# Top-32 attention and two MLPs on one core: more buffers for raw weights, shared memory for two stages, one more mask on ScalarE

## The chip, the cores and the metric

The kernel runs on 1 core of one Trainium2 chip. The metric is the device time of one execution in microseconds (us), the median of several runs. Below, PE is TensorE's matmul, PEld its weight load, DVE is VectorE, ACT is ScalarE, POOL is GpSimd and SP is SyncE, which issues the DMAs here.

## The reference

```python
# q, k, v: (4 batches, 8 heads, 576, 64); w_in: 512x2048, w_out: 2048x512, twice
scores = (q @ k^T) / 8
kth = the 32nd largest score of each row
attn = softmax of the scores >= kth, the others left out
x = (attn @ v), heads side by side: 2304 x 512
h = x @ w_in;  x = (h - tanh(h)) @ w_out
h = x @ w2_in; out = where(h > 0, h, exp(min(h, 0)) - 1) @ w2_out
```

## The kernel before

The 2304 tokens are six chunks of 384 (`CHUNKS`). Attention of a chunk is cut into 8 groups of three 128-row score tiles: chunk 0 is groups 0 to 7, chunk 1 groups 8 to 15, chunk 2 groups 16 to 23. A tile's top 32 are found on VectorE by four MAX8 (`find`, line 395) with three MATCH_REPLACE8 between them (`drop`, line 409). Then the mask: for most tiles ScalarE has taken the exponentials early (line 399) and VectorE multiplies them by `score >= 32nd` and sums (line 416, SCALAR_TENSOR_TENSOR). For the first `MASK_ACT[chunk]` tiles of a group ScalarE does it alone instead: after GpSimd has made two small constants (lines 401 to 403), a Prelu with a huge slope (line 411) and an Exp that sums (line 412). Before, that is three of three tiles in chunk 0, one in chunk 1, none later.

The two MLPs work in fp32r with each operand as a high and a low part, so every weight is prepared once. `prepare` loads 128x512 int64 words of raw weights (`wr`, 4 KB a partition, `RAW_BUFS` buffers). ScalarE reads them twice (lines 189 and 190), GpSimd once (line 192), VectorE joins the pieces (`wf`, line 195), ScalarE and GpSimd split that into high and low (`wp`, lines 142 and 143), and a DMA stores the pair to DRAM (line 200). There are 64 such halves: (MLP 0 or 1, 16 blocks, in or out). Blocks 12 to 21 (`EARLY`) are stored and read back, the others are used at once by chunk 0 too; later chunks read all from DRAM (line 211). While attention of chunk 0 runs, the first 26 halves take a PSUM bank for one piece (`"wide" in stage`), and the other 38 do not.

An MLP step is `first` (12 matmuls into `h`, line 566), tanh or exp on ScalarE, `gate` (VectorE, lines 580 and 585; then `gh` on ScalarE and `gl` on GpSimd, lines 142 and 143) and `second` (9 matmuls into three `acc` banks, line 602). Chunk c's steps run beside attention of chunk c+1.

Attention scores of chunk 2 are made ahead, in the stretch before the first MLP step. For 24 tiles `park` makes the scores on PE (`pp`, line 360), ScalarE copies them (`sp`, line 343, two buffers) and a DMA takes them to DRAM (`sd`, line 345). All 24 must be through before the first `h`, and before the first two transposes of chunk 0's last group (`hurried`), because `bank("h")` first closes the PSUM pool of `pp`.

Everything is written in program order by ticks, four to a group, and a list scheduler then sets the order on each engine by simulated time and priority. Each engine runs its own list strictly in order. Parks carry a low priority (`PARK_LOW`).

Of the kernel before, what the change touches and what calls it, by code (L numbers as in the profile page):

```python
# [19 lines left out]
P = 128  # L20
B, H, S, D = 4, 8, 576, 64
# [7 lines left out]
NF = DFF // P  # L29
# [13 lines left out]
SIZES = [sum(n for _, _, n in c) for c in CHUNKS]  # L43
NMAX = max(SIZES)

MASK_ACT = [3, 1, 0, 0, 0, 0]

GATE_GP = [0, 0, 1, 1, 1, 2]

# [19 lines left out]
PARK_BUFS = 2  # L69
# [18 lines left out]
G_BUFS = 3  # L88
T_BUFS = 3
# [9 lines left out]
NU = 384  # L99
# [8 lines left out]
def tile_topk_attention_two_mlps(  # L108
# [58 lines left out]
    weights, loads = {}, [(ci, m, ft) for ci in range(len(SIZES)) for m in range(2) for ft in range(NF)]  # L167

    def weight_tile(half, name):
        return sb.tile([P, 2, 512], F32R, tag=f"w{half}", name=name, bufs=(WI_BUFS, WO_BUFS)[half])  # L170

    stage = {"at": 0, "wide": True}

    def prepare(m, ft, half):

        raw = sb.tile([P, 512], I64, tag="wr", name=f"wr{m}_{ft}_{half}", bufs=RAW_BUFS)
        nc.sync.dma_start(raw, (w1, w2)[m][ft][:, half * 512 : half * 512 + 512])  # L180
        words = raw.bitcast(F32).rearrange("p (n w) -> p n w", w=2)
        w = sb.tile([P, 512], F32, tag="wf", name=f"wf{m}_{ft}_{half}", bufs=2)
        low, scaled = words.bitcast(U32)[:, :, 0], words[:, :, 1]
        small = scaled
        if "wide" in stage:
            small = bank(f"acc{stage['at'] % 3}", f"sc{m}_{ft}_{half}", 1)
            stage["at"] += 1
        if small is not scaled:
            nc.scalar.activation(small, scaled, copy, scale=2.0**-112)
        nc.scalar.activation(low.bitcast(I32), low, copy, scale=2.0**-29 * (1 - 2.0**-20), bias=-0.5 + 7.5 * 2.0**-20)  # L190
# [4 lines left out]
        nc.vector.scalar_tensor_tensor(  # L195
            w.bitcast(U32), small.bitcast(U32), 3, low, op0=ALU.logical_shift_left, op1=ALU.bitwise_or
        )
        wt = weight_tile(half, f"wp{m}_{ft}_{half}")
        split(wt[:, 0], wt[:, 1], w)
        nc.sync.dma_start(f(scratch[m, ft, half]), f(wt))  # L200
        return wt

    def load_next():
        if loads:
            ci, m, ft = loads.pop(0)
            for half in range(2):
                if ci == 0 and m * NF + ft not in EARLY:
                    weights[ci, m, ft, half] = prepare(m, ft, half)
# [13 lines left out]
    for ci, size in enumerate(SIZES):  # L222
        for p in range(NPAIR):
            row = []
            c0 = 0
            for b, q0, n in CHUNKS[ci]:
                for heads in ([[0], [1]] if n >= 256 else [[0, 1]]):
                    u = Unit()
# [10 lines left out]
            cuts, k = [], 0  # L239
# [7 lines left out]
            for us in cuts:  # L247
                g = Group()
# [19 lines left out]
    def parked(u):  # L268

        return u.g.at in PARK  # L270

    pair_k = {}

    def wide(u):

        return u.whole or parked(u)

    def load_q(u):
        if wide(u):
            h = u.heads[0]  # L280
            tag, bufs = ("qp", 1) if parked(u) else ("qraw", QR_BUFS)
            u.qraw = sb.tile([P, NU], F32, tag=tag, name=f"qw{u.id}", bufs=bufs)
            nc.gpsimd.memset(u.qraw[(1 - h) * D : (2 - h) * D, : u.n], 0.0)
            nc.sync.dma_start(u.qraw[h * D : h * D + D, : u.n], qT[u.b, 2 * u.p + h, :, u.q0 : u.q0 + u.n])
            return
        u.qraw = sb.tile([P, NU], F32, tag="qraw", name=f"qraw{u.id}", bufs=QR_BUFS)
        src = qT[u.b, 2 * u.p + u.heads[0] : 2 * u.p + u.heads[-1] + 1, :, u.q0 : u.q0 + u.n].rearrange("h d s -> d h s")
        nq = u.n * len(u.heads)
        for half in range(2):
            nc.sync.dma_start(u.qraw[half * D : half * D + D, :nq].rearrange("d (h s) -> d h s", s=u.n), src)  # L290

# [263 lines left out]
    def first(ci, m, ft):  # L555
        n = SIZES[ci]
        xh, xl = x_tiles[ci] if m == 0 else z_tiles[ci]
        h = bank("h", f"h{ci}_{m}_{ft}", 2)[:, :n]
        wv = weights.pop((ci, m, ft, 0)).rearrange("p a (k c) -> p a k c", c=P)
        jobs = [(wi, xs, kt) for wi, xs in ((0, xh), (1, xh), (0, xl)) for kt in range(4)]  # L560
        if m == 0 and ft == 0:
            jobs.sort(key=lambda x: x[2])
        late = (n // P - 1) * P
        for cs in (slice(0, late), slice(late, n)) if m == 1 and ft < PARTED and late else (slice(0, n),):
            for a, (wi, xs, kt) in enumerate(jobs):
                nc.tensor.matmul(h[:, cs], wv[:, wi, kt], xs[:, kt, cs], start=(a == 0), stop=(a == len(jobs) - 1))  # L566
# [152 lines left out]
    early = list(EARLY)  # L719
    for tick in range(FIRST_TICK, n_ticks):  # L720
# [18 lines left out]
        at, r = divmod(tick, 4)  # L739
# [63 lines left out]
```

## Time and profile before

| what | us |
|---|---|
| median of 3 runs (1238.9 to 1240.79) | 1240.16 |
| the profiled execution | 1244.14 |
| its span, first to last instruction | 1242.4 |
| PE busy in the span | 1156.3 (93%) |
| PEld | 981.6 (79%) |
| DVE | 973.8 (78%) |
| ACT | 761.9 (61%) |
| POOL | 584.3 (47%) |

Busy time is the union of an engine's instructions. Each engine's share changes from stage to stage: PE's is low up to about 186 us, where the first MLP steps begin, and DVE's falls to nearly nothing from 1055 us, when attention is done. A matmul's record reaches from its issue to its end and overlaps its neighbours, so a PE that is busy all the time can still be waited for in small pieces.

### The profile page before, as it was taken

How to read it: one execution, taken by the hardware profiler on the slowest of the kernel's cores; microseconds unless marked ns; L12 is line 12 of the kernel's file. 1: busy time of each engine (PE TensorE's matmuls, PEld its weight loads, DVE VectorE, ACT ScalarE, POOL GpSimd, SP SyncE). 2: the span in 40 equal slices, each digit the busy share in tenths (PEclk: the TensorE clock that was granted, in tenths of full speed). 3: DMA queues.
4: the chain of work that ended last, by engine and by line, in shares of the span. 5: the costliest groups of instructions: out<-in, count | busy, mean ns of one | idle time of the engine just before them, and what ended most of it. 6: DMA issues, size and time to landing. Idle time of an engine off the chain costs nothing.

```text
span 1242.4 us, 19713 instructions
## 1 busy us (share of the span) xinstructions
PE 1156.3 (93%) x6349; PEld 981.6 (79%) x6349; DVE 973.8 (78%) x1951; ACT 761.9 (61%) x1646; POOL 584.3 (47%) x629
## 2 busy tenths in 40 slices
PE   6577669999889999999999999999999999999998
PEld 4344358888778887988888989989998988889887
DVE  6989989999999999969879679899789997100111
ACT  5899987787885435645556556566565564432333
POOL 4677758965975222244423345435244413333221
PEclk8788788999999999999999999999999999999999
DMA  7899947795779986778857779787778766687672
GB/s 244 313 318 339 300 147 243 255 364 185 269 273 381 310 240 186 249 222 251 238 180 231 238 227 262 209 277 215 242 239 252 197 163 199 205 282 252 219 251 80
DMA packets 115464, 302.83 MB, mean 244 GB/s; under 512 B 22560, under 2 KB 39840, under 8 KB 115360
## 3 DMA queue, kind: packets, MB, share of 16 engines
q1 hardware_dynamic: 115360, 301.56, 76.9%
q8 instruction: 51, 0.84, 0.3%
q14 instruction: 53, 0.43, 0.1%
HBM read 256.11 MB, written 45.39 MB: 243 GB/s over the span
## 4 chain that ended last, share of the span: by engine, by line
PE 70%; DMA 9%; ACT 8%; DVE 7%; POOL 2%; issue 2%; SPq 1%; ACTq 0%; POOLq 0%; DVEq 0%
PE h L566 28%; PE acc L602 28%; DMA wr<-in_w_dram 6%; PE av L459 5%; PE pt L437 4%; DVE vm L395 3%; DVE w L409 2%; PE ps L372 2%; PE ps L373 2%; DVE wf L195 1%; PE ps L360 1%; ACT s L374 1%; DVE e L416 1%; ACT wr L190 1%; POOL wr L192 1%
## 5 line engine op out<-in xcount | busy, mean ns | idle before, releaser
L143 POOL TENSOR_TENSOR gl<-g,gh 128x384 fp32r<-128x384 f32 x192 | 204.1, 1065 | 360.5 <-ACT gh L142 343.7
L395 DVE MAX8 vm<-w 128x8 f32<-128x576 f32 x432 | 317.3, 749 | 2.9
L602 PE MATMUL acc<-wt,gh 128*128 128x512 f32 x1020 | 271.6, 397 | 0.8 <-ACT gh L142 0.8
L602 PEld LDWEIGHTS acc<-wt,gh 128*128 128x128 f32 x1020 | 187.2, 188 | 36.2 <-issue 2.7
L409 DVE MATCH_REPLACE8 w<-vm,w 128x576 f32<-128x576 f32 x288 | 213.0, 741 | 0.0
L580 DVE SCALAR_TENSOR_TENSOR g<-t,h 128x384 f32<-128x384 f32 x96 | 52.3, 545 | 126.8 <-ACT t L572 124.4
L566 PE MATMUL h<-zh,wt 128*128 128x384 f32 (+2 forms) x784 | 148.0, 324 | 2.3 <-ACT zh L621 1.5
L602 PE MATMUL acc<-wt,gl 128*128 128x512 f32 x510 | 149.6, 398 | 0.0
L142 ACT ACTIVATE gh<-g 128x384 fp32r<-128x384 f32 x192 | 100.5, 525 | 74.6 <-DVE g L580 38.4
L566 PE MATMUL h<-xh,wt 128*128 128x384 f32 x672 | 142.1, 339 | 1.9 <-DVE g L580 1.5
L566 PEld LDWEIGHTS h<-zh,wt 128*128 128x128 f32 x784 | 126.7, 188 | 8.8 <-ACT zh L621 2.7
L438 ACT ACTIVATE ph<-pt 116x384 f32<-116x384 f32 (+1 forms) x240 | 110.2, 496 | 34.0 <-PE pt L437 33.3
L395 DVE MAX8 vm<-s 128x8 f32<-128x576 f32 x144 | 106.8, 750 | 29.6 <-ACT s L374 29.1
L374 ACT ACTIVATE s<-ps 128x288 f32<-128x288 f32 (+1 forms) x272 | 105.7, 415 | 38.0 <-PE ps L373 30.7
L437 PE MATMUL pt<-ident,e 128*116 128x128 f32 (+1 forms) x720 | 114.1, 286 | 14.7 <-ACT e L412 6.0
L566 PEld LDWEIGHTS h<-xh,wt 128*128 128x128 f32 x672 | 117.6, 188 | 8.8 <-DVE g L580 1.8
L571 ACT ACTIVATE t<-h 128x384 f32<-128x384 f32 x96 | 46.7, 488 | 118.3 <-PE h L566 116.3
L437 PEld LDWEIGHTS pt<-ident,e 128*116 128x116 f32 (+1 forms) x720 | 88.2, 140 | 35.8 <-ACT e L412 9.7
L416 DVE SCALAR_TENSOR_TENSOR e<-s,vm,e 128x576 f32<-128x576 f32 x115 | 111.8, 980 | 2.7 <-ACT e L399 2.2
L569 ACT ACTIVATE t<-h 128x384 f32<-128x384 f32 x96 | 47.0, 491 | 104.5 <-PE h L566 104.4
L602 PEld LDWEIGHTS acc<-wt,gl 128*128 128x128 f32 x510 | 93.6, 188 | 18.5 <-POOL gl L143 0.2
L409 DVE MATCH_REPLACE8 w<-vm,s 128x576 f32<-128x576 f32 x144 | 106.6, 741 | 0.0
(84 smaller groups left out, 2001.4 us busy)
## 6 DMA issues: line engine op xcount, KB each, us to landing
wt<-w SPq DMA_DIRECT2D x340, 512.0 KB, 4.9
wr<-in_w_dram SPq DMA_DIRECT2D x64, 512.0 KB, 5.7
w<-wp SPq DMA_DIRECT2D x64, 512.0 KB, 5.3
kraw<-in_kT_dram SPq DMA_DIRECT2D x96, 144.0 KB, 4.7
vraw<-in_vL_dram SPq DMA_DIRECT2D x64, 160.0 KB, 3.7
sd<-sp SPq DMA_DIRECT2D x24, 288.0 KB, 4.9
s<-sd SPq DMA_DIRECT2D x24, 288.0 KB, 6.7
qraw<-in_qT_dram SPq DMA_DIRECT2D x64, 96.0 KB, 4.0
```

Source lines behind the costliest of these rows:

```text
L142: nc.scalar.activation(hi, src, copy)
L143: return nc.gpsimd.tensor_sub(lo, src, f(hi))
L374: nc.scalar.activation(s[lo:hi, cs], pt[lo:hi, :HS], copy)
L395: nc.vector.max(g.vm[:, j, min(r, 1)], u.s[t] if r == 0 else g.w[j])
L409: nc.vector.match_replace(g.w[j], v, u.s[t] if r == 0 else g.w[j], FILL)
L416: nc.vector.scalar_tensor_tensor(u.e[t], u.s[t], v[:, 7:8], u.e[t], op0=ALU.is_ge, op1=ALU.mult, accum_out=g.sum[:, j : j + 1])
L437: nc.tensor.transpose(pt[:kn, j * P : j * P + P], v.e[t][:, k0 : k0 + kn], ident)
L438: nc.scalar.activation(g.ph[:kn, blk, :nq], pt[:kn, :nq], copy)
L459: nc.tensor.matmul(banks[c0][h * D : h * D + D, : v.n], v.vraw[h][:kn, blk], v.g.ph[:kn, blk, cs], start=(blk == order[0]), stop=(blk == o ...
L566: nc.tensor.matmul(h[:, cs], wv[:, wi, kt], xs[:, kt, cs], start=(a == 0), stop=(a == len(jobs) - 1))
L580: nc.vector.scalar_tensor_tensor(g, t, -1.0, h, op0=ALU.add, op1=ALU.max)
L602: nc.tensor.matmul(acc[ci, m][t], gx[:, t * P : t * P + P], wt[:, wi], start=(ft == 0 and k == 0), stop=(ft == NF - 1 and k == 2),)
```

## The change

Three things. `RAW_BUFS` goes from 3 to 5. To make room, tiles that only live before the first MLP step (`qp`, `kp`, `sp`) move to a pool of their own, which is closed when the first MLP tile is asked for; a pool with the MLP's `t`, `g`, `gh` and `gl` then takes the same memory. And `MASK_ACT[1]` goes from 1 to 2. `OPEN_BUFS` is 0, so its branch is never taken, and `prepare` is cut into three functions that issue the same instructions.

```diff
-MASK_ACT = [3, 1, 0, 0, 0, 0]
+MASK_ACT = [3, 2, 0, 0, 0, 0]
+OPEN_BUFS = 0
-RAW_BUFS = 3
+RAW_BUFS = 5
...
+    opening = ExitStack()
+    pools = {"open": opening.enter_context(tc.tile_pool(name="op", bufs=1))}
+
+    def mlp_tile(shape, dt, **kw):
+        if "open" in pools:
+            opening.close()
+            del pools["open"]
+            pools["mlp"] = pool("mlp", 1)
+        return pools["mlp"].tile(shape, dt, **kw)
...
-            u.qraw = sb.tile([P, NU], F32, tag=tag, name=f"qw{u.id}", bufs=bufs)
+            u.qraw = (pools["open"] if parked(u) else sb).tile([P, NU], F32, tag=tag, name=f"qw{u.id}", bufs=bufs)
...
-        s = sb.tile([P, S], F32, tag="sp", name=f"sp{u.id}_{t}", bufs=PARK_BUFS)
+        s = pools["open"].tile([P, S], F32, tag="sp", name=f"sp{u.id}_{t}", bufs=PARK_BUFS)
...
-        t = sb.tile([P, NMAX], F32, tag="t", name=f"t{ci}_{m}_{ft}", bufs=T_BUFS)[:, :n]
+        t = mlp_tile([P, NMAX], F32, tag="t", name=f"t{ci}_{m}_{ft}", bufs=T_BUFS)[:, :n]
```

(`kp` is changed as `qp` is, and `g`, `gh` and `gl` as `t` is.) The scheduler answers with another order up to about the end of chunk 2's attention; behind that each engine's list is the same as before. Three places show it. Line numbers of the change's rows are those of the changed file.

SP, the first raw loads (`wr0_13_0` is MLP 0, block 13, half 0; `sd` are the parks' stores). Before:

```order
L325 DMA vraw0_1_0_0_0_0_497<-in_vL_dram 128x320
L180 DMA wr0_13_0_502<-in_w1_dram 128x512
L325 DMA vraw0_1_0_0_1_1_701<-in_vL_dram 128x320
L284 DMA qw0_1_0_0_0_212<-in_qT_dram 64x384
L345 DMA sd2_0_1_192_0_0_291<-sp2_0_1_192_0_0_286 128x576
L345 DMA sd2_0_1_192_0_1_324<-sp2_0_1_192_0_1_319 128x576
L180 DMA wr0_13_1_514<-in_w1_dram 128x512
```

Now:

```order
L352 DMA vraw0_1_0_0_0_0_500<-in_vL_dram 128x320
L195 DMA wr0_13_0_505<-in_w1_dram 128x512
L195 DMA wr0_13_1_517<-in_w1_dram 128x512
L195 DMA wr0_14_0_624<-in_w1_dram 128x512
L352 DMA vraw0_1_0_0_1_1_704<-in_vL_dram 128x320
L311 DMA qw0_1_0_0_0_215<-in_qT_dram 64x384
L372 DMA sd2_0_1_192_0_0_294<-sp2_0_1_192_0_0_289 128x576
L372 DMA sd2_0_1_192_0_1_327<-sp2_0_1_192_0_1_322 128x576
L195 DMA wr0_14_1_636<-in_w1_dram 128x512
```

Two raw loads more are issued ahead of the first parks' stores. With the loads the joins on VectorE move up: the join of `wf0_5_1`, the 35th half of the list, stands 206th in VectorE's list before and 182nd now, and still 36 halves are joined before the first MLP gate in both.

PE, at the transposes of chunk 0's last group (`pt0_3_0_3_0_0_1_0` and `..._1_1` are its blocks 0 and 1, `pp2_3_1_192_1_2` is the last park). Before, the last park stands at row 171, 29 rows ahead of block 0:

```order
L372 MATMUL ps1_0_0_384_0_0_0_0_1335<-kk1_0_0_384_0_0_1234,qs1_0_0_384_0_1231 128x288
L373 MATMUL ps1_0_0_384_0_0_0_0_1335<-kk1_0_0_384_0_0_1234,qs1_0_0_384_0_1231 128x288
L372 MATMUL ps1_0_0_384_0_0_1_0_1339<-kk1_0_0_384_0_0_1234,qs1_0_0_384_0_1231 128x288
L373 MATMUL ps1_0_0_384_0_0_1_0_1339<-kk1_0_0_384_0_0_1234,qs1_0_0_384_0_1231 128x288
L437 MATMUL pt0_3_0_3_0_0_1_0_1563<-ident_69,e0_3_0_0_1_0_1370 116x128
L437 MATMUL pt0_3_0_3_0_0_1_1_1568<-ident_69,e0_3_0_0_1_0_1370 116x128
L437 MATMUL pt0_3_0_3_0_0_1_2_1573<-ident_69,e0_3_0_0_1_0_1370 116x128
```

Now:

```order
L387 MATMUL pp2_3_1_192_1_2_1459<-kw2_3_1_192_0_1037,qw2_3_1_192_1_1152 128x288 x2
L399 MATMUL ps1_0_0_384_0_1_1_1_1396<-kk1_0_0_384_0_1_1240,qs1_0_0_384_0_1234 128x288
L400 MATMUL ps1_0_0_384_0_1_1_1_1396<-kk1_0_0_384_0_1_1240,qs1_0_0_384_0_1234 128x288
L464 MATMUL pt0_3_0_3_0_0_0_3_1402<-ident_72,e0_3_0_0_0_0_1155 116x128
L464 MATMUL pt0_3_0_3_0_0_0_3_1402<-ident_72,e0_3_0_0_0_1_1156 116x128
L464 MATMUL pt0_3_0_3_0_0_0_3_1402<-ident_72,e0_3_0_0_0_2_1157 116x128
L464 MATMUL pt0_3_0_3_0_0_0_4_1407<-ident_72,e0_3_0_0_0_0_1155 112x128
L464 MATMUL pt0_3_0_3_0_0_0_4_1407<-ident_72,e0_3_0_0_0_1_1156 112x128
L464 MATMUL pt0_3_0_3_0_0_0_4_1407<-ident_72,e0_3_0_0_0_2_1157 112x128
L464 MATMUL pt0_3_0_3_0_0_1_0_1566<-ident_72,e0_3_0_0_1_0_1373 116x128
```

The last park now stands 9 rows ahead of block 0, and the last three parks, which stood between rows 159 and 171, stand between rows 197 and 223 of a list whose first MLP matmul is row 242 before and 243 now. On ACT the last park's copy is row 285 now and the first tanh row 314.

ACT, the mask of a group of chunk 1 (`e1_3_1_0_0_0` is its tile 0, `_1` and `_2` the others). Before:

```order
L399 ACTIVATE e1_3_1_0_0_1_3861<-s1_3_1_0_0_1_3530,mb1_3_1_3_1_0_0_3793 128x576
L399 ACTIVATE e1_3_1_0_0_2_3862<-s1_3_1_0_0_2_3622,mb1_3_1_3_1_0_0_3793 128x576
L411 ACTIVATE e1_3_1_0_0_0_3860<-s1_3_1_0_0_0_3457,nk1_3_1_3_1_0_0_3999 128x576
L473 ACTIVATE xun1_2_3764<-av1_2_0_3765 128x192
L142 ACTIVATE gh0_1_9_3823<-g0_1_9_3821 128x384
L194 ACTIVATE wr1_12_0_3658<-wr1_12_0_3658 128x512
L190 ACTIVATE wr1_12_1_3669<-wr1_12_1_3669 128x512
L142 ACTIVATE wp1_11_1_3598<-wf1_11_1_3593 128x512
L412 ACTIVATE e1_3_1_0_0_0_3860,sum1_3_1_3_1_0_0_3794<-e1_3_1_0_0_0_3860,b21_3_1_3_1_0_0_4000 128x576
```

Now:

```order
L426 ACTIVATE e1_3_1_0_0_2_3869<-s1_3_1_0_0_2_3628,mb1_3_1_3_1_0_0_3800 128x576
L438 ACTIVATE e1_3_1_0_0_0_3867<-s1_3_1_0_0_0_3464,nk1_3_1_3_1_0_0_4005 128x576
L438 ACTIVATE e1_3_1_0_0_1_3868<-s1_3_1_0_0_1_3536,nk1_3_1_3_1_0_0_4005 128x576
L152 ACTIVATE wp1_12_0_3671<-wf1_12_0_3669 128x512
L210 ACTIVATE wr1_14_0_3845<-wr1_14_0_3845 128x512
L500 ACTIVATE xun1_2_3771<-av1_2_0_3772 128x192
L152 ACTIVATE gh0_1_8_3718<-g0_1_8_3716 128x384
L439 ACTIVATE e1_3_1_0_0_0_3867,sum1_3_1_3_1_0_0_3801<-e1_3_1_0_0_0_3867,b21_3_1_3_1_0_0_4006 128x576
L439 ACTIVATE e1_3_1_0_0_1_3868,sum1_3_1_3_1_0_0_3801<-e1_3_1_0_0_1_3868,b21_3_1_3_1_0_0_4006 128x576
```

Tile 1 loses its early Exp and gains a Prelu and a summing Exp. Over chunk 1 VectorE's list is 8 masks shorter and ScalarE's 8 instructions longer. In both orders the raw weights stand between them (now two blocks further on).

## Rows read from the trace of the kernel before

**Rows 1.** Busy time by stretch: length, then PE, PEld, DVE, ACT, POOL, granted clock, DMA share, GB/s

```profile
31.00:155.00 124.00, 82.82 (x311) 50.44 (x312) 115.60 (x231) 114.66 (x248) 90.91 (x108) 0.79 0.93 318
155.00:186.00 31.00, 21.18 (x110) 16.65 (x107) 26.43 (x54) 25.35 (x60) 17.50 (x18) 0.83 0.46 146
186.00:403.00 217.00, 201.49 (x1194) 175.11 (x1195) 214.17 (x399) 166.84 (x351) 166.98 (x163) 0.97 0.81 281
403.00:527.00 124.00, 122.27 (x686) 103.40 (x685) 122.47 (x266) 61.41 (x133) 31.70 (x42) 1.00 0.82 247
527.00:1055.00 528.00, 526.13 (x3070) 462.45 (x3069) 453.74 (x927) 310.27 (x689) 210.10 (x226) 1.00 0.77 226
```

**Rows 2.** What DVE waited for, 186 to 403 us: total, times, longest

```profile
DVE g L585 <- ACT t L569: 1.0, 1, 1.0
```

**Rows 3.** What DVE waited for, 0 to 186 us

```profile
DVE vm L395 <- ACT s L374: 7.9, 5, 5.6
DVE wf L195 <- POOL wp L143: 6.6, 2, 3.4
DVE wf L195 <- POOL wr L192: 5.1, 4, 2.7
```

**Rows 4.** DVE groups by line: 186 to 420 us (MAX8, the masks), then 420 to 1055

```profile
L395 DVE MAX8 vm<-w 128x8 f32<-128x576 f32 x93 | 67.3, 743 | 0.1
L416 DVE SCALAR_TENSOR_TENSOR e<-s,vm,e 128x576 f32<-128x576 f32 x24 | 31.1, 1308 | 0.6 <-ACT e L399 0.6
L416 DVE SCALAR_TENSOR_TENSOR e<-s,vm,e x24: 772/1464/1986, 185.2 to 419.7; 128x576 f32<-128x576 f32 x24
...
L416 DVE SCALAR_TENSOR_TENSOR e<-s,vm,e 128x576 f32<-128x576 f32 x88 | 77.6, 888 | 1.7 <-ACT e L399 1.1
L416 DVE DVE_READ_ACCUMULATOR e<-s,vm,e 128x1 f32 x88 | 7.1, 81 | 0.0
```

**Rows 5.** ScalarE's masks, groups by line, 186 to 403 us

```profile
L412 ACT ACTIVATE e<-e,b 128x576 f32<-128x576 f32 x7 | 5.4, 773 | 0.5 <-ACT e L411 0.4
L411 ACT ACTIVATE e<-s,nk 128x576 f32<-128x576 f32 x7 | 5.4, 766 | 0.0
L412 ACT ACTIVATION_READ_ACCUMULATOR e<-e,b 128x1 f32 x7 | 1.3, 191 | 0.0
```

**Rows 6.** Timelines of ACT, DVE and PE: start, length, in brackets the wait ahead

```profile
27.73 0.63 ACT L189 ACTIVATE sc<-wr 128x512 f32<-128x512 f32 x1 [2.91 <-DMA wr<-in_w_dram]
31.56 0.69 DVE L195 SCALAR_TENSOR_TENSOR wf<-sc,wr 128x512 uint32<-128x512 uint32 x1 [3.23 <-POOL wp L143]
159.41 0.66 ACT L190 ACTIVATE wr<-wr 128x512 int32<-128x512 uint32 x1 [2.87 <-DMA wr<-in_w_dram]
161.49 0.67 ACT L190 ACTIVATE wr<-wr 128x512 int32<-128x512 uint32 x1 [1.42 <-DMA wr<-in_w_dram]
163.00 0.61 PE L372 MATMUL ps<-kk,qs 128*128 128x288 f32 x1 [5.09 <-ACT ph L438]
166.17 0.69 DVE L195 SCALAR_TENSOR_TENSOR wf<-wr 128x512 uint32<-128x512 uint32 x1 [3.37 <-POOL wp L143]
```

**Rows 7.** What ACT waited for, 0 to 186 us, and SP's DMA queue, 0 to 420 us

```profile
ACT sc L189 <- DMA wr<-in_w_dram: 11.9, 5, 3.0
...
SPq L180 <- DVE wf L195: 37.5, 23, 4.3
```

**Rows 8.** The parks' tiles: durations min/median/max, first and last start; landing of their stores

```profile
L360 PE MATMUL pp<-kw,qw x96: 406/462/848, 9.3 to 136.1; 128*128 128x288 f32 x96
L343 ACT ACTIVATE sp<-pp x24: 625/652/742, 13.9 to 139.8; 128x576 f32<-128x576 f32 x24
DMA to landing us min/median/max: 2.1/4.9/7.9
```

**Rows 9.** PE's timeline at the first MLP matmuls

```profile
169.62 0.90 PE L566 MATMUL h<-xh,wp 128*128 128x384 f32 x2
```

**Rows 10.** Busy time of one stretch, columns as in the first group

```profile
372.00:403.00 31.00, 29.53 (x173) 26.00 (x170) 31.00 (x65) 18.41 (x36) 18.06 (x17) 1.00 0.98 371
```

More of the change, by code (lines that the diff above doesn't have):

```diff
@@ L170, in weight_tile, with words_of @@
         return sb.tile([P, 2, 512], F32R, tag=f"w{half}", name=name, bufs=(WI_BUFS, WO_BUFS)[half])
-    stage = {"at": 0, "wide": True}
+    stage = {"at": 0, "wide": True, "raw": -1}
     def prepare(m, ft, half):
-        raw = sb.tile([P, 512], I64, tag="wr", name=f"wr{m}_{ft}_{half}", bufs=RAW_BUFS)
+        early = "wide" in stage
+        at = stage["raw"] = stage["raw"] + 1
+        if early and at % (RAW_BUFS + OPEN_BUFS) >= RAW_BUFS:
+            raw = pools["open"].tile([P, 512], I64, tag="wo", name=f"wr{m}_{ft}_{half}", bufs=OPEN_BUFS)
+        else:
+            raw = sb.tile([P, 512], I64, tag="wr", name=f"wr{m}_{ft}_{half}", bufs=RAW_BUFS)
         nc.sync.dma_start(raw, (w1, w2)[m][ft][:, half * 512 : half * 512 + 512])
+        words_of(m, ft, half, raw)
+    def words_of(m, ft, half, raw):
         words = raw.bitcast(F32).rearrange("p (n w) -> p n w", w=2)
-        w = sb.tile([P, 512], F32, tag="wf", name=f"wf{m}_{ft}_{half}", bufs=2)
         low, scaled = words.bitcast(U32)[:, :, 0], words[:, :, 1]
         small = scaled
-        if "wide" in stage:
+        early = "wide" in stage
+        if early:
             small = bank(f"acc{stage['at'] % 3}", f"sc{m}_{ft}_{half}", 1)
             stage["at"] += 1
-        if small is not scaled:
-            nc.scalar.activation(small, scaled, copy, scale=2.0**-112)
-        nc.scalar.activation(low.bitcast(I32), low, copy, scale=2.0**-29 * (1 - 2.0**-20), bias=-0.5 + 7.5 * 2.0**-20)
+        if True:
+            if small is not scaled:
+                nc.scalar.activation(small, scaled, copy, scale=2.0**-112)
+            nc.scalar.activation(low.bitcast(I32), low, copy, scale=2.0**-29 * (1 - 2.0**-20), bias=-0.5 + 7.5 * 2.0**-20)
         top = raw.bitcast(FP16).rearrange("p (n w) -> p n w", w=4)[:, :, 1]
@@ L194, in prepare, with join @@
             nc.scalar.activation(scaled, scaled, copy, scale=2.0**-112)
-        nc.vector.scalar_tensor_tensor(
-            w.bitcast(U32), small.bitcast(U32), 3, low, op0=ALU.logical_shift_left, op1=ALU.bitwise_or
-        )
+        join(m, ft, half, small, low)
+    def join(m, ft, half, small, low):
+        w = sb.tile([P, 512], F32, tag="wf", name=f"wf{m}_{ft}_{half}", bufs=2)
+        if True:
+            nc.vector.scalar_tensor_tensor(
+                w.bitcast(U32), small.bitcast(U32), 3, low, op0=ALU.logical_shift_left, op1=ALU.bitwise_or
+            )
         wt = weight_tile(half, f"wp{m}_{ft}_{half}")
+        if m * NF + ft not in EARLY:
+            weights[0, m, ft, half] = wt
         split(wt[:, 0], wt[:, 1], w)
         nc.sync.dma_start(f(scratch[m, ft, half]), f(wt))
-        return wt
     def load_next():
@@ L207, in load_next @@
                 if ci == 0 and m * NF + ft not in EARLY:
-                    weights[ci, m, ft, half] = prepare(m, ft, half)
+                    prepare(m, ft, half)
                     continue
@@ L295, in load_k @@
                 tag, bufs = ("kp", 1) if parked(u) else ("kraw", KR_BUFS)
-                k = pair_k[u.ci, u.p] = sb.tile([P, S], F32, tag=tag, name=f"kw{u.id}", bufs=bufs)
+                k = pair_k[u.ci, u.p] = (pools["open"] if parked(u) else sb).tile([P, S], F32, tag=tag, name=f"kw{u.id}", bufs=bufs)
                 for h in range(2):
@@ L577, in gate @@
         h, t = parts[ci, m, ft]
-        g = sb.tile([P, NMAX], F32, tag="g", name=f"g{ci}_{m}_{ft}", bufs=T_BUFS)[:, :n]
+        g = mlp_tile([P, NMAX], F32, tag="g", name=f"g{ci}_{m}_{ft}", bufs=T_BUFS)[:, :n]
         if m == 1:
@@ L585, in gate @@
             nc.vector.tensor_sub(g, h, t)
-        gh = sb.tile([P, NMAX], F32R, tag="gh", name=f"gh{ci}_{m}_{ft}", bufs=G_BUFS)[:, :n]
-        gl = sb.tile([P, NMAX], F32R, tag="gl", name=f"gl{ci}_{m}_{ft}", bufs=G_BUFS)[:, :n]
+        gh = mlp_tile([P, NMAX], F32R, tag="gh", name=f"gh{ci}_{m}_{ft}", bufs=G_BUFS)[:, :n]
+        gl = mlp_tile([P, NMAX], F32R, tag="gl", name=f"gl{ci}_{m}_{ft}", bufs=G_BUFS)[:, :n]
         newest["gates"] = split(gh, gl, g)
```

## The prediction

> **What bounds the kernel now.** I read the busy time by stretch first, then who waited for whom in each stretch, then single tiles. From 527 us on PE is the bound: it is busy 526.13 of 528 us, while DVE is at 454 [rows 1]. Behind the end of chunk 2's attention the change leaves every engine's list as it was, so that part can only be moved as a whole. What counts is how early it begins.
>
> From 186 to 403 us, which is chunk 0's MLP beside chunk 1's attention, DVE is the bound: busy 214.17 of 217 us, next to no wait [rows 1, 2]. PE has slack there. Its weight loads take 175.11 us; in the stretch from 527 us, where PE waits for nobody, they fill 462.45/528 = 87.6% of the time. At that density 175.11 us would fit into 200 us. So 17 us could be taken out of these 217 before PE becomes the bound. From 403 to 527 us the two are close: DVE 122.47 of 124, PE's loads 103.40, which would fit into 118.
>
> Up to 186 us nobody is full for all the time, but DVE is nearest: from 31 to 155 us it is busy 115.60 of 124, ACT 114.66, and the DMA engines 93% [rows 1]. Of DVE's waits up to 186 us the largest is the start (5.6 of the 7.9 for scores). The others are waits to join raw weights: 6.6 and 5.1, together 11.7 us [rows 3]. Every us that DVE gains up to 403 us lets the first MLP steps, and all behind them, come a us earlier, up to PE's slack.
>
> **Part 1, the masks.** Chunk 1 has 8 groups, each loses one mask on DVE. From 186 to 420 us a mask takes 1308 ns in the mean, later 888 [rows 4]. Its shortest is 772 in this stretch and its median 1464, so most of the difference is waiting inside the instruction, while POOL is busy 167 of 217 us against 210 of 528 later [rows 1]. With a mask goes the reading of its sum, 81 ns, which I leave off because neighbouring instructions overlap a little: 8 x 1308 = **10.5 us less on DVE**. The ends are 8 x 772 = 6.2 us, if the waiting only moves to DVE's next instruction, and 8 x 1986 = 15.9 us. I take the mean, because a mask that meets a POOL instruction in progress waits for the rest of it, and what stands behind a mask on DVE is mostly a MAX8 or its like, which took 743 ns in the mean in this stretch, with no such stretching [rows 4].
>
> The Trainium skill weighs in here ("SBUF — State Buffer", SBUF: two separate sides): a DVE instruction with two SBUF inputs and a GpSimd instruction that reads SBUF take a shared port pair as an exclusive lock, and the second is blocked until the first is done. Read strictly, an instruction with two SBUF inputs behind the removed mask, a join of weights above all, would inherit the wait; by that the term would be 6.2 instead of 10.5.
>
> **Part 2, what ScalarE takes over.** The early Exp of the tile becomes a summing Exp of about the same length, so each group adds a Prelu and the reading of a sum, 766 + 191 ns [rows 5]: 8 x 957 = 7.7 us. ACT is idle 50 of the 217 us [rows 1], so this lies beside DVE's work. But ACT works in order: behind a mask that waits for GpSimd's two constants stand the tanh and `gh` of an MLP step, for which DVE's gate and PE wait, and the next transposes on PE now wait for a mask on ACT for two tiles instead of one. Bounds: nothing, and all 7.7 us. I take 2 us, nearer to nothing since DVE waited 1.0 us for ACT's tanh in all this stretch [rows 2]. GpSimd's constants cover two columns instead of one in as many instructions; I put that at nothing, covered by POOL's 50 idle us.
>
> **Part 3, five raw buffers.** A load of raw weights is issued when the join that last read the buffer is done: SP's queue stood 37.5 us in 23 waits for just that [rows 7]. The load then takes its way, and ACT, in order, stands in front of it: 11.9 us for the first of its two readings alone [rows 7]. Two of these are plain in the timeline. At 27.73 and at 159.41 ACT had waited 2.91 and 2.87 us for a load, and 1.42 more at 161.49; behind that came the join on DVE that had waited 3.23 (31.56) and 3.37 us (166.17), and at 163.00 PE had waited 5.09 us for copies behind the same stall [rows 6]. With two buffers more, a load is issued when the join two places further back is done. Before, 35 joins stand in 206 rows of DVE's list, one in 6 rows or about 4 us at 743 ns a row; two are 8 us, more than any of these waits. So I take 3.23 + 3.37 = 6.6 us as gone.
>
> Against it: the scheduler places the joins earlier too, the 35th by 24 rows of DVE's list, or 24 x 0.74 = 18 us. The DMA engines have 7% of 124 us = 8.7 us free from 31 to 155 [rows 1], so preparation cannot come 18 us earlier there; up to 18 - 8.7 = 9 us of waits for a join can return. The same number of halves is joined ahead of the first gate as before. Bounds of the part: 11.7 us gained, 9 us lost. I take 6.6 gained and 2.7 of the 9 returned, less than a third, since a late join holds DVE only when nothing is left ahead of it: **3.9 us less**.
>
> **Part 4, the moved parks and the shared memory.** The last three parks now stand just ahead of the transposes of chunk 0's last group. Before, the last copy of a park began at 139.8 us and the first MLP matmul at 169.62 [rows 8, 9], 30 us of cover. Now there are 9 PE rows. I cost it at nothing because in ACT's and PE's lists the scheduler has left work between the parks, and the other late link, the mask sums of that group, is on DVE; without that cover it is the second rival below. The first MLP tiles wait for the last store of `sp`, 4.9 us in the median [rows 8]; between that copy and the first tanh ACT's list has 28 instructions, some 11 us at half the length of a Prelu [rows 5]. Nothing, then, and 7.9 - 4.9 = 3 us if the store is slow.
>
> **The sum.** -10.5 + 2 - 3.9 = -12.4 us. Against the profiled execution's 1244.14 that is 1231.7; it ran 4.0 us longer than the median of the runs shown, 1240.16, to which the forecast applies: **1228**. It needs 8.5 us of PE's 17 us slack in the stretch and the rest ahead of it. Its own range is 1221 to 1234. About 0.2% (2.5 us) is what a measurement of this kernel can tell from no change, so faster means below 1237.7 and slower above 1242.6.
>
> **The rivals.** *Masks only.* The raw buffers change nothing: DMA at 93% from 31 to 155 us says that loads issued earlier only queue longer; for it also speaks that weight tiles and `wf` keep their buffers. Against it: from 372 to 403 us the engines moved 371 GB/s at 98%, against 318 in that stretch [rows 10, 1]. Time: 1240.2 - 10.5 + 2 = 1231.7, or 1229 to 1236 with the lost end of part 3 taken at half. The Trainium skill ("DMA: Bandwidth & Descriptors", Where 436 GB/s comes from) puts one core's HBM limit near 358 GB/s; by it 11% would be free at 318 GB/s, an estimate of 14 us in 124, and the measured 371 is above that page's figure.
>
> *ScalarE becomes the bound of chunk 1.* The wait inside the mask moves on (6.2 us), ACT's 7.7 us land half on the path (3.9), nothing in part 3: 1240.2 - 2.3 = 1238, from 1236 to 1240. For it: ACT's work stands in front of every gate. Against it: 77% busy.
>
> *Late parks, slower.* `sp` has two buffers, so a park's copy on ACT waits for the store of the park two ahead. That store lands in up to 7.9 us [rows 8]. Three parks in a row, with the loads of raw weights queued in the same DMA engines: if two of the copies wait 7.9 us each, ACT stands 16 us in order, with the exponentials and copies of chunk 0's last group behind it, and DVE runs out of tiles. -12.4 + 16 = +3.6: 1244, and up to 1251 if the third waits too. It decides from a delay of 12.4 us. For it: low priority has pushed the parks to the end of the list. Against it: from 155 to 186 us the DMA engines are at 46% [rows 1], so the stores should land quickly.
>
> **How the numbers follow.** Forecast 52%, masks only 20%, ScalarE 13%, late parks 15%. All of the first two are faster; of the third, 5 points are faster and 8 the same; of the last, 1 the same and 14 slower. Faster 0.77, same 0.09, slower 0.14. The range reaches from 1218, the forecast with part 3 at 11.7 us and the masks a little above the mean, to 1243; it leaves out most of the late parks.
>
> **What would show it.** Right: 8 fewer masks on DVE and ScalarE's Prelu up by 8; ACT's wait for raw loads up to the first MLP step well below half of what it was; DVE's waits for joins down by some 4 us; the first MLP gate some 4 us earlier; DVE still busy for almost all of the chunk-1 stretch, that stretch about 8 us shorter, and everything from chunk 3 on shifted and unchanged. Wrong: idle time on DVE in the chunk-1 stretch that ends on ACT or POOL; a gap on PE just ahead of the first `h` that ends on `sp`; waits of DVE for joins above 12 us.

## The result, and the profile after the change

The changed kernel takes 1228.17 us (median of 4 runs, 1227.65 to 1229.57) against 1240.47 for the kernel before (4 runs): a ratio of 0.9901, 95% interval 0.9886 to 0.9916, or 12.3 us less. The forecast was 1228. Its profiled execution took 1228.12 us, so its trace stands for the median; that of before stood for 1244.14, and the two traces differ by 16 us where the medians differ by 12.3. What one pair of traces shows is therefore checked below against others with the same lists.

Busy time by stretch after the change, columns as in [rows 1]:

```profile
31.00:155.00 124.00, 86.10 (x311) 51.19 (x312) 121.11 (x236) 120.85 (x260) 98.82 (x113) 0.78 0.94 337
155.00:186.00 31.00, 25.17 (x130) 19.81 (x128) 29.18 (x60) 25.60 (x59) 16.36 (x20) 0.89 0.39 128
186.00:403.00 217.00, 209.72 (x1268) 181.09 (x1267) 211.74 (x403) 171.85 (x367) 162.57 (x160) 0.99 0.86 290
403.00:527.00 124.00, 121.71 (x680) 103.09 (x678) 115.80 (x249) 59.57 (x129) 34.84 (x42) 1.00 0.78 242
527.00:1055.00 528.00, 526.09 (x3078) 463.23 (x3076) 444.42 (x912) 312.52 (x693) 208.10 (x223) 1.00 0.77 226
```

From 31 to 155 us DVE and ACT are now both full (121 of 124, against 115.6 and 114.7). From 186 to 403 us PE has risen from 201.5 to 209.7, and DVE is no longer without waits: its idle time there has gone from 2.8 to 5.3 us. Most of it ends on ACT and POOL, which the prediction had named as a sign of being wrong:

```profile
DVE vm L422 <- ACT s L401: 2.4, 2, 1.9
DVE r L517 <- POOL r L514: 1.2, 1, 1.2
```

From 403 us DVE's load has fallen from 122.5 to 115.8 of 124 while PE stayed at 122: there PE is the bound, as light01 shows below.

What DVE waited for (0 to 186 us, the joins), what ACT waited for, and SP's queue (0 to 420 us), to be held against [rows 3] and [rows 7]:

```profile
DVE wf L221 <- POOL wp L153: 2.1, 4, 0.9
...
DVE wf L221 <- POOL wr L212: 0.3, 1, 0.3
```

```profile
ACT sc L209 <- DMA wr<-in_w_dram: 4.1, 2, 3.7
```

```profile
SPq L195 <- DVE wf L221: 33.4, 24, 3.6
```

DVE's waits for joins fell from 11.7 to 2.4 us, ACT's for raw loads from 17.8 to 4.1. SP's queue still stands 33.4 us behind the joins (37.5 before): the buffers hardly shortened that, but DVE and ACT wait far less behind it.

The DVE groups from 186 to 420 us, and the distribution of the masks there, against [rows 4]:

```profile
L221 DVE SCALAR_TENSOR_TENSOR wf<-wr 128x512 uint32<-128x512 uint32 x31 | 35.9, 1157 | 0.6 <-POOL wp L153 0.6
L443 DVE SCALAR_TENSOR_TENSOR e<-s,vm,e 128x576 f32<-128x576 f32 x18 | 17.4, 985 | 0.0
```

```profile
L443 DVE SCALAR_TENSOR_TENSOR e<-s,vm,e x18: 770/816/1576, 203.8 to 410.1; 128x576 f32<-128x576 f32 x18
```

The masks that stayed on DVE also became shorter: 985 ns in the mean instead of 1308, with a median of 816 instead of 1464 (from the end of chunk 0's attention to its first output 1052 instead of 1410 in the mean). That was not forecast.

Two more lines for the parks: the last one is now made on PE at 159.9 us instead of 136.1 [rows 8], and PE waits for its copy just ahead of the first MLP matmul (at 164.33 us instead of 169.62, [rows 9]).

```profile
L387 PE MATMUL pp<-kw,qw x96: 403/588/850, 9.3 to 159.9; 128*128 128x288 f32 x96
```

```profile
162.62 0.87 PE L464 MATMUL pt<-ident,e 128*116 128x128 f32 x6 [0.56 <-ACT sp L370]
```

That wait is 0.56 us long; the only longer one of PE on a late park, ahead of another park's scores, is 1.0 us. The late parks cost next to nothing.

### The profile page after: what moved, and what is told of

Same layout as the page of the kernel before. It is cut to its first block, busy times and chain, and to the rows that moved or that the text cites. A ratio compares the mean times of both kernels' runs of the same rounds, so it can differ in the third digit from the quotient of the medians.

```text
span 1226.3 us, 19738 instructions
## 1 busy us (share of the span) xinstructions
PE 1156.4 (94%) x6349; PEld 978.0 (80%) x6349; DVE 963.9 (79%) x1935; ACT 767.7 (63%) x1662; POOL 586.9 (48%) x629
## 4 chain that ended last, share of the span: by engine, by line
PE 74%; DVE 9%; DMA 5%; ACT 5%; POOL 3%; issue 2%; SPq 1%; ACTq 0%; DVEq 0%; POOLq 0%
PE h L593 30%; PE acc L629 30%; PE av L486 5%; PE pt L464 4%; DVE vm L422 4%; DVE w L436 3%; DMA wr<-in_w_dram 3%; PE ps L399 2%; PE ps L400 2%; DVE wf L221 2%; DMA w<-wp 1%; POOL wr L212 1%; POOL wp L153 1%; ACT y L643 1%; ACT s L401 1%
## 5 line engine op out<-in xcount | busy, mean ns | idle before, releaser
L153 POOL TENSOR_TENSOR gl<-g,gh 128x384 fp32r<-128x384 f32 x192 | 208.6, 1087 | 376.3 <-ACT gh L152 355.5
L443 DVE SCALAR_TENSOR_TENSOR e<-s,vm,e 128x576 f32<-128x576 f32 x107 | 95.5, 902 | 2.4 <-ACT e L426 1.3
```

Source lines behind the costliest of these rows:

```text
L443: nc.vector.scalar_tensor_tensor(u.e[t], u.s[t], v[:, 7:8], u.e[t], op0=ALU.is_ge, op1=ALU.mult, accum_out=g.sum[:, j : j + 1])
```

## The experiments

Times are medians in us; "before" in a ratio is the kernel before in the same set of runs (1239.4 to 1240.5). Three places are compared between traces: the end of chunk 0's attention (where DVE begins `xl`, the low part of its last piece), chunk 0's first output (its DMA on SP's queue) and chunk 1's. The two stretches between them hold chunk 1's and chunk 2's attention.

| kernel | raw buffers, ahead / behind | masks on ACT in chunk 1 | us | ratio to before (95%) |
|---|---|---|---|---|
| pool_only | 3 / 3, shared memory | 1 | 1241.36 | 1.0013 (1.0002 to 1.0024) |
| mask_only | 3 / 3, old memory | 2 | 1238.00 | 0.9981 (0.9970 to 0.9992) |
| raw4 | 4 / 4 | 2 | 1235.31 | 0.9969 (0.9955 to 0.9983) |
| raw_only | 5 / 5 | 1 | 1232.12 | 0.9932 (0.9921 to 0.9944) |
| the change | 5 / 5 | 2 | 1228.17 | 0.9901 (0.9886 to 0.9916) |
| early5 | 5 / 3 | 1 | 1234.77 | 0.9955 (0.9943 to 0.9966) |
| late5 | 3 / 5 | 1 | 1245.92 | 1.0046 (1.0031 to 1.0061) |
| open1 | 6 / 5 | 2 | 1237.44 | 0.9986 (0.9974 to 0.9999) |
| mask3 | 5 / 5 | 3 | 1243.97 | 1.0032 (1.0019 to 1.0045) |

### One part at a time

**The masks alone.** In the kernel before:

```diff
-MASK_ACT = [3, 1, 0, 0, 0, 0]
+MASK_ACT = [3, 2, 0, 0, 0, 0]
```

> The kernel before with two of three masks of chunk 1 on ScalarE, three raw buffers and the old memory. Up to the end of chunk 0's attention all lists are those of before. A, the terms of the prediction (masks -10.5 + 2 us, buffers -3.9): 1240.5 - 8.5 = 1232, remaining masks on DVE about 1300 ns each. B, the buffers carried most (after the change the first MLP gate came 7.2 us earlier in the traces, 188.68 to 181.48, which masks of chunk 1 cannot do): 12.3 - 7.2 = 5.1 us are left for the masks, 1235.4. C, the masks alone carry it: 1228 to 1229.

Measured: 1238.0, 2.4 us less by the ratio (1.0 to 3.7). All three theories put it lower. Busy time of mask_only and of pool_only (whose lists are those of before) from the end of chunk 0's attention to chunk 0's output:

```profile
176.49:386.85 210.36, 196.09 (x1188) 172.16 (x1189) 201.63 (x381) 176.60 (x379) 167.03 (x163) 0.97 0.83 280
```

```profile
179.65:393.82 214.17, 198.11 (x1186) 170.69 (x1185) 209.69 (x398) 169.28 (x359) 170.83 (x163) 0.98 0.82 274
```

DVE's busy time falls by 8.1 us (the sum had 10.5, with 6.2 as its lower end), the stretch by 3.8: DVE's idle time rises from 4.5 to 8.7 us. Of that, 5.9 us end on ScalarE, against 3.5 in pool_only; the two largest waits in mask_only are

```profile
DVE vm L395 <- ACT s L374: 2.5, 2, 2.1
DVE g L585 <- ACT t L569: 1.7, 1, 1.7
```

In the next stretch (172.61 us against 171.02) 1.6 us are given back. The trace of mask_only is of an execution of 1235.1 us, 2.9 under its median.

**The buffers alone.** In the changed kernel, the other way round:

```diff
-MASK_ACT = [3, 2, 0, 0, 0, 0]
+MASK_ACT = [3, 1, 0, 0, 0, 0]
```

> The changed kernel with one of three masks of chunk 1 on ScalarE as before: five raw buffers and the shared memory alone. Up to the end of chunk 0's attention all lists are those of the changed kernel. A: 1240.5 - 3.9 = 1236.6. B: 1240.5 - 7.2 = 1233.3. C: 1240 or a little more. First MLP gate as in the changed kernel, 181 to 182 us, by all three; what differs is how much of it is kept up to the end.

Measured: 1232.12, 8.4 us less by the ratio (6.9 to 9.8), twice the forecast's 3.9. B, that the buffers carry most, is what happened. The two parts alone sum to 10.8 us; with both it is 12.3, a difference within the intervals.

**The shared memory alone.** Three buffers and one mask in the changed kernel:

```diff
-MASK_ACT = [3, 2, 0, 0, 0, 0]
+MASK_ACT = [3, 1, 0, 0, 0, 0]
...
-RAW_BUFS = 5
+RAW_BUFS = 3
```

> The changed kernel with three raw buffers and one mask on ScalarE: the shared memory alone. All five lists are those of before, row by row, so only addresses and the waits of first users differ. A and B: 1240.5, within 0.2%. D, the first tanh stands behind the last park's store or the memory costs elsewhere: up to 3 us more, with a wait on sd or sp in front of the first tanh on ACT. Its trace is also a second look at the lists of before: if its first gate lies near 185 us instead of 188.7, part of the 7.2 us belongs to that one profiled execution (4 us longer than the median) and not to the buffers.

Measured: 1241.36, 1.6 us more than before by the ratio (0.2 to 3.0), under what is told from no change here, and no wait on a park stands in front of the first tanh. Its first `gh` starts at 188.3 us, against 189.2 in the trace of before: the late gate there is no accident of one execution. One trace is not exact, though: mask_only has the same lists up to the end of chunk 0's attention and reached it at 176.5 us, pool_only at 179.7, before at 180.5.

**Four buffers.**

```diff
-RAW_BUFS = 5
+RAW_BUFS = 4
```

> The changed kernel with four raw buffers. A: a load is issued one join earlier than before (about 4 us of DVE's list), which covers the two waits of 3.2 and 3.4 us, so nearly all of the buffers' part is there: 1229 to 1229.5. B, it takes the depth: half of the buffers' part is missing, 1230 to 1232, and ACT's wait for raw loads up to 186 us stands between 17.8 (three buffers) and 4.1 us (five).

Measured: 1235.31. Even B was too hopeful: with two masks, going from three to four gives 2.7 us by the medians and 1.5 by the ratios, from four to five 7.1 and 8.4. ACT's waits for raw loads up to 180 us are 7.1 us there, most of the way from 17.8 to 4.1, but chunk 0's attention ends at 177.09 us, less than half of the way that five buffers bring it (below). That is one trace, of an execution 2.4 us above the median; but the time too says that the wait alone doesn't tell what a buffer is worth.

### Where the buffers pay

Five buffers for the halves prepared beside chunk 0's attention, three behind (`OPEN_BUFS` in the code is just that):

```diff
-MASK_ACT = [3, 2, 0, 0, 0, 0]
+MASK_ACT = [3, 1, 0, 0, 0, 0]
...
-OPEN_BUFS = 0
+OPEN_BUFS = 2
...
-RAW_BUFS = 5
+RAW_BUFS = 3
```

> One mask on ScalarE as before; five raw buffers for the 26 halves prepared beside chunk 0's attention, three for the 38 after them. Up to there the lists are those of the kernel with five buffers throughout (1232.1), three throughout gave 1240.2 to 1241.4. A, the prediction's account (the buffers take waits for loads away ahead of the first MLP step, nothing after it): nearly all of the gain, 1232 to 1234. E, by the stretches of the traces (about 4.3 us gained up to the end of chunk 0's attention, 5.6 in chunk 1's): half of it, 1236 to 1237, with the end of chunk 0's attention near 174.5 us as with five buffers and the stretch from there to the first output near 214 us as with three.

The mirror image, three ahead and five behind (also with one mask and `RAW_BUFS = 3`):

```diff
-        if early and at % (RAW_BUFS + OPEN_BUFS) >= RAW_BUFS:
-            raw = pools["open"].tile([P, 512], I64, tag="wo", name=f"wr{m}_{ft}_{half}", bufs=OPEN_BUFS)
+        if not early and at % 5 >= RAW_BUFS:
+            raw = mlp_tile([P, 512], I64, tag="wx", name=f"wr{m}_{ft}_{half}", bufs=2)
```

> The mirror image: one mask on ScalarE, three raw buffers for the first 26 halves, five for the 38 after them (the two more lie with the MLP's tiles). Up to VectorE's row 182 the lists are those of before. A: little, 1239 to 1241. E: 1235 to 1237, with the end of chunk 0's attention near 179 us as before and the stretch from there to the first output near 210 us instead of 215. F, the two act together only (a late load delays the next in either stretch): both halves give less than half each, both near 1238 to 1239.

early5: 1234.77, 5.6 us less by the ratio (4.2 to 7.1), two thirds of what five buffers throughout give, between A and E. late5: 1245.92, 5.7 us more than before, which no theory had. So five behind are worth 2.8 us once five stand ahead, and in late5, the one kernel with five behind and three ahead, they gain nothing. The traces agree on the first part: chunk 0's attention ends at 176.5, 179.7 and 180.5 us in mask_only, pool_only and before, whose lists are alike almost to there, and at 172.0 to 174.6 in the eight that prepare with five buffers under that stretch: 5.5 us earlier in the mean (178.9 and 173.4). The stretch behind it is about as long with three buffers behind (early5, first line) as before (214.2 us in pool_only, 216.9 in before), and 6 us shorter with five (raw_only, second). Since early5 began it 2.5 us earlier, its first output comes 3.5 us later, near the 2.8 of the times:

```profile
172.01:387.97 215.96, 200.35 (x1195) 174.32 (x1195) 210.82 (x397) 170.06 (x360) 172.46 (x164) 0.97 0.82 270
```

```profile
174.56:384.44 209.88, 197.41 (x1182) 171.90 (x1181) 207.01 (x394) 165.62 (x353) 169.26 (x161) 0.96 0.84 284
```

Why late5 is slower stays open: its order is another one from VectorE's row 182 on, its stretch took 217.42 us with DVE busy for 213.40, and the next one 174.89 against 171.08 before.

### What takes the masks' worth

**ScalarE's work.** The second tile's mask left out: a summing early Exp alone, so that tile's outputs are unmasked and ScalarE keeps no Prelu for it.

```diff
+        free = 1 if by_act == 2 else -1
...
             if r == 1 and j >= by_act:
                 nc.scalar.activation(u.e[t], u.s[t], AF.Exp, bias=g.mb[:, j : j + 1], scale=SCALE)
+            if r == 1 and free == j:
+                nc.scalar.activation(
+                    u.e[t], u.s[t], AF.Exp, bias=g.mb[:, j : j + 1], scale=SCALE, accum_out=g.sum[:, j : j + 1]
+                )
...
+            elif j == free:
+                pass
             elif j < by_act:
```

> The changed kernel with the second tile's mask in chunk 1 left out: a summing early Exp alone, so VectorE's list keeps its 8 masks fewer and ScalarE loses 8 Prelus (8 x 0.77 = 6.2 us) and all waits for the second tile's constants; that tile's outputs are not masked. A, the prediction's 2 us for ScalarE's extra work: 1226. G, ScalarE's place in order ate half of the masks' worth (alone they gave 2.2 us of the 8.5 to 10.5 that VectorE was relieved of): 1222 to 1224. P, PE is full from 360 us on after the change and takes the rest: 1227 to 1229, no gain.

Measured: 1231.19, 3.0 us more than the changed kernel, with 6 us less work on ScalarE in the stretch. None of the three theories had that. DVE's idle time in the stretch stayed (5.5 us, 5.3 after the change), so nothing speaks for G, that the 8 Prelus eat the masks' worth. But taking work away cost 3 us, so the new order of the lists moved the time by at least that, and a gain of that size could be hidden under it: G isn't ruled out.

**One dose more.**

```diff
-MASK_ACT = [3, 2, 0, 0, 0, 0]
+MASK_ACT = [3, 3, 0, 0, 0, 0]
```

> The changed kernel with all three masks of chunk 1's tiles on ScalarE: 8 masks less on VectorE once more, 8 Prelus and sums more on ScalarE (7.7 us on top of 171.85 busy of 217). A, VectorE still bounds the stretch: 1228.2 - 8.5 = 1220 down to 1224 if PE's slack of some 8 us runs out. G: ScalarE eats as much as VectorE gains: 1227 to 1230. P, PE bounds: 1227 to 1229. A slower result, 1231 or more, would say that ScalarE has become the bound.

Measured: 1243.97, 15.8 us more than the changed kernel. Here ScalarE's place in order does bite. What DVE waited for from 172.14 to 394.98 us, and the largest wait on DVE, ACT and PE:

```profile
DVE vm L422 <- ACT s L401: 7.3, 3, 6.3
DVE g L607 <- ACT t L599: 4.0, 2, 2.8
```

```profile
286.42 0.76 DVE L422 MAX8 vm<-s 128x8 f32<-128x576 f32 x1 [6.27 <-ACT s L401]
```

```profile
280.80 2.11 ACT L438 ACTIVATE e<-s,nk 128x576 f32<-128x576 f32 x3
282.81 0.76 ACT L439 ACTIVATE e<-e,b 128x576 f32<-128x576 f32 x1
...
285.64 0.69 ACT L401 ACTIVATE s<-ps 128x288 f32<-128x288 f32 x2
```

```profile
282.55 0.30 PE L400 MATMUL ps<-kk,qs 128*128 128x288 f32 x1
```

PE had the scores that DVE wants ready at 282.85. ScalarE, in order, first finishes three Prelus, two of their sums and some copies, and copies the scores at 285.64. DVE, with no other tile, stands for 6.27 us.

**PE.** In chunk 0's MLP the products with the gate's low part are left out for all but the last step, with one mask (light1) and two (light2):

```diff
-        jobs = [(k, t) for k in range(3) for t in range(nt)]
+        jobs = [(k, t) for k in range(3) for t in range(nt) if k < 2 or ci or ft == NF - 1]
```

> Five raw buffers, one mask of chunk 1 on ScalarE, and in chunk 0's MLP the products with the low part of the gate left out for all but the last step: 15 x 2 x 3 = 90 matmuls less on PE between the first gate and chunk 0's output, some 26 us of weight loads and moves. With all of PE's work this kernel took 1232.1. If VectorE bounds chunk 1's stretch, 1230 to 1232 (only PE's part of the late idle comes back); if PE takes a share of the bound, 1226 to 1230.

> The same with two masks of chunk 1 on ScalarE; with all of PE's work 1228.2, 3.9 us less than with one mask. P, with masks gone PE is the next bound and takes what VectorE gains: with PE light the second mask is worth the full 8 x 1.08 - 1.6 = 7 us, so 7 us below light1. G, ScalarE's place in the order takes it: 3 to 4 us below light1 as with all of PE's work, with VectorE's idle time in the stretch (5.3 us after the change) ending on ScalarE.

Measured: 1228.51 and 1223.40, 3.6 and 4.8 us less than with all of PE's work (2.7 and 3.7 by the ratios): PE has a part in the bound of chunk 1's stretch. With PE light, DVE is idle there for 0.04 and 0.9 us, where raw_only and the change had 2.9 and 5.3. The second mask is worth 5.1 us instead of 3.9, between P and G, but that difference is no larger than the scatter of these few runs. Then the same in chunk 1's MLP as well, beside chunk 2's attention:

```diff
-        jobs = [(k, t) for k in range(3) for t in range(nt) if k < 2 or ci or ft == NF - 1]
+        jobs = [(k, t) for k in range(3) for t in range(nt) if k < 2 or ci > 1 or ft == NF - 1]
```

> As light2 (two masks on ScalarE, five raw buffers), with the products of the gate's low part left out in chunk 1's MLP too, the one that runs beside chunk 2's attention: 90 matmuls less on PE there, 26 to 27 us at the rate of a PE that waits for nobody. In light2 VectorE was idle 12.5 of the 170.6 us from chunk 0's to chunk 1's output, PE 2.6. If PE took there what the masks give VectorE, chunk 1's output comes 12 to 13 us earlier, then VectorE is full and bounds: 1211 with the rest of the 27 us as new idle time on PE, or less where VectorE's lead lets PE catch up. If VectorE's idle time there is ScalarE's doing, it stays near 12 us, and the time falls by 5 us at most, 1218 or more. PE bound to the end and VectorE never: 1196 to 1198.

Measured: 1211.36, 12.0 us below light2, as expected if PE bounds there. From chunk 0's output to chunk 1's, the changed kernel, light2 and light01:

```profile
380.85:552.04 171.19, 168.90 (x934) 143.76 (x933) 153.25 (x328) 83.20 (x179) 51.96 (x61) 1.00 0.79 239
```

```profile
376.78:547.34 170.56, 167.99 (x926) 142.03 (x925) 158.10 (x339) 83.90 (x184) 50.62 (x62) 1.00 0.79 244
```

```profile
375.01:531.13 156.12, 148.34 (x830) 126.64 (x829) 150.24 (x318) 81.48 (x176) 53.45 (x60) 0.99 0.90 273
```

This stretch took 171.08 us before and 171.19 after, with DVE idle for 12 us and then for 18. In the thirteen traces with all of PE's work in it, it takes 169.9 to 176.3 us. With that work cut it falls to 156 us, and DVE is idle for 6. So PE bounds it near 170 us, and a VectorE with less to do can't shorten it below that. A kernel like light01 with one mask was not run: how much of the masks' worth comes out once PE is light in both stretches isn't measured.

**A sixth buffer ahead.**

```diff
-OPEN_BUFS = 0
+OPEN_BUFS = 1
```

> The changed kernel with a sixth raw buffer for the halves prepared beside chunk 0's attention, in memory that the MLP's tiles take later. If depth went on paying as from four to five (7 us): 1223 to 1225. After the change ScalarE is busy 20.00 of 20 us in each of the four slices from 40 to 120 us and waits only 4.1 us for raw loads up to 186 us, so: within 2 us of 1228.2, 3 us less at best.

Measured: 1237.44, 9.3 us more than the change. Chunk 0's attention ends at 180.28 us, 6 later: in VectorE's list 11 rows more stand ahead of it, nearly all MAX8 and MATCH_REPLACE of chunk 1, some 8 us at 0.74. The first MLP step waits for them, and in the stretch that follows DVE is idle for 14 us:

```profile
180.28:392.05 211.77, 198.30 (x1165) 170.80 (x1164) 197.38 (x365) 166.90 (x357) 161.28 (x156) 0.95 0.83 279
```

Of the kernels that leave no work out, none is faster than the change itself.

## Why the prediction was right

The time was right to 0.2 us, and so were the direction and the places where the gain was sought. But that the sum fell on the measured time is luck: two of its terms were wrong by like amounts in opposite directions.

- **Part 3, the buffers: -3.9 forecast, -8.4 measured alone.** Up to the first MLP step the mechanism held: the two named waits are gone, DVE's waits for joins fell by 9.3 us. Part of it came back in another shape than the forecast's. The joins of the second form, with both inputs in SBUF (those of the first 26 halves take one from PSUM), took 1314 ns each up to 186 us, against 690 before (the two lines below, before and after), 5 us in all for eight; seven of the eight start while GpSimd is at work, three of the seven before. The net, 4.3 us, is near the 3.9; over more traces the end of chunk 0's attention comes 5.5 us earlier, and early5, which has this part alone, gained 5.6. The failed step is what followed: with five buffers behind as well, the stretch of chunk 1 gains too (2.8 us more than early5), where the forecast saw no waits and so no gain.

```profile
L195 DVE SCALAR_TENSOR_TENSOR wf<-wr 128x512 uint32<-128x512 uint32 x7 | 4.8, 690 | 3.4 <-POOL wp L143 3.4
```

```profile
L221 DVE SCALAR_TENSOR_TENSOR wf<-wr 128x512 uint32<-128x512 uint32 x8 | 10.5, 1314 | 0.0
```

- **Part 1 and 2, the masks: -10.5 + 2 = -8.5 forecast, -2.4 alone, -3.9 with five buffers.** VectorE was relieved by about 8 us instead of 10.5: its busy time in the whole execution is 969.7 us in pool_only and 961.7 in mask_only, 971.6 in raw_only and 963.9 after the change. The larger miss, and the failed step, is the price of what that lets through, put at 2 us: DVE's idle time grew by 4 us in mask_only's stretch and by 2.4 between raw_only and the change, and PE bounds the next one. "It needs 8.5 us of PE's 17 us slack" measured that slack in chunk 1's stretch by the density of weight loads. From 403 to 527 us, in chunk 2's stretch, the same measure gave 6 us (103.40 us of loads that would fit into 118 of 124), and there was none: the length of that stretch did not change (171.08 and 171.19 us), until PE's work was cut. How the missing 4.6 to 6.1 us divide between PE, ScalarE's place in order and the new order of the lists stays open.
- The rival in which ScalarE becomes the bound gave the masks -2.3 us alone, close to the 2.4 measured, but it gave the buffers nothing, and for its reason there is no clear evidence at this dose: taking ScalarE's extra work away gained nothing. The reason comes true one mask later, in mask3.
- **Part 4** held: PE's longest wait on a late park was 1.0 us, and the late-parks rival is out. **Masks only** is out as well: the buffers without the mask gained 8.4 us, and the DMA engines moved 337 GB/s from 31 to 155 us against 318.
- What "the buffers" gained includes the order that the scheduler makes for them. Five buffers in the order of before were not run, and mask_free, open1 and late5 show that another order can cost 3 to 9 us. That part 3's gain comes from the waits, and not from the order, is therefore argued: ahead of the first MLP step the waits are seen to go, behind it the cause of the gain stays open.
- From chunk 1's output on nothing changed but the start: SP's last stores start at 1238.03 and 1222.00 us, 669.56 and 669.96 us behind chunk 1's.

## What to carry to other kernels

Work taken off the busiest engine is worth at most what the next engine lets through, stretch by stretch: measure the slack of the next bound in every stretch that the gain has to pass, and distrust a slack computed from another stretch's density. A buffer more in front of an in-order chain can be worth more than the waits it removes, and one more after that can be worth less than nothing where a list scheduler turns it into another order. When a forecast of two parts comes true, run the parts: here each was off by a factor of two or more.

## What was not expected of the hardware

**A join or a mask that starts while GpSimd is at work takes longer.** DVE and POOL in one piece of the changed kernel:

```profile
304.06 0.68 DVE L221 SCALAR_TENSOR_TENSOR wf<-wr 128x512 uint32<-128x512 uint32 x1
...
308.03 0.80 DVE L443 SCALAR_TENSOR_TENSOR e<-s,vm,e 128x576 f32<-128x576 f32 x1
...
311.00 1.80 DVE L221 SCALAR_TENSOR_TENSOR wf<-wr 128x512 uint32<-128x512 uint32 x1 [0.62 <-POOL wp L153]
```

```profile
304.08 0.74 POOL L428 TENSOR_SCALAR nk<-vm 128x2 f32<-128x2 f32 x1
...
308.13 1.58 POOL L153 TENSOR_TENSOR gl<-g,gh 128x384 fp32r<-128x384 f32 x1
...
310.93 1.39 POOL L212 TENSOR_TENSOR wr<-wr,tiny 128x512 f16<-128x512 f32 x1
```

The join at 304.06 starts ahead of a two-column POOL instruction and takes 0.68 us; that instruction takes 0.74, where the same one took 0.22 at 171.07 us. The join at 311.00 starts 0.07 us after a POOL product and takes 1.80, ending 0.48 us behind that product's end. The mask at 308.03 starts first and is on time, and POOL's `gl` behind it takes 1.58 us instead of 1.0. Counted over the timelines from 181 to 400 us in before, pool_only, mask_only, raw_only, raw4 and the change: joins that start while POOL has nothing in progress (leaving overlaps under 0.02 us aside) take 0.67 to 0.68 us in the mean (2 to 5 of 31 in each), the others 1.05 to 1.21; masks 0.80 to 1.02 and 1.20 to 1.54. This is the exclusive lock that the Trainium skill describes ("SBUF — State Buffer", SBUF: two separate sides), in both directions. The trace agrees with it in kind and nearly in size: by a full block the join would have ended 0.68 us behind the product instead of 0.48, and `gl` 1.0 us behind the mask instead of 0.88. The joins that take one input from PSUM do not stretch: of the 26 before, 21 start while POOL is at work, and none takes over 0.70 us. The strict reading in the prediction, that the joins inherit all that the masks shed, does not hold: with the second mask gone, the 31 joins of the stretch went from 1107 to 1157 ns, 1.6 us of the 8.1 that the masks shed between raw_only and the change, and with three buffers they did not grow at all (1022 ns in pool_only, 990 in mask_only).

**The masks wait less with five buffers behind.** In chunk 1's stretch the masks left on DVE take 1220 to 1410 ns in the mean in the five kernels with three or four raw buffers behind, and 972 to 1178 in those with five. Fewer of them start while POOL is at work (12 of 22 in raw_only against 15 of 20 before). In early5 and raw_only, whose times differ by 2.8 us, the 20 masks of the stretch take 24.3 and 21.6 us. That this is what five buffers behind are worth was not tried, nor why the order falls so.

**The scatter.** Kernels with three or four buffers ahead spread by 4.1 to 6.6 us over their runs (6 to 25 each). Those with five spread by 1.4 to 2.7 (4 or 5 each), except mask3, which spreads by 6.8 in nine runs, like open1 with six buffers in twelve. Fewer runs spread less (four of the kernel before by 2.3), so that the buffers narrow the scatter is not shown.
